# Attention by pairs of heads, with plain fp32 products on halves of TensorE

## The chip, the cores and the metric

The kernel runs on one core of one Trainium2 chip. The metric is the device time of one execution in microseconds (us). "Clock" is the clock that TensorE was granted, as a share of 2.4 GHz; its lower level is 0.5 (1.2 GHz).

## The reference, cut to what matters

Three stages follow each other: causal attention with a memory term, a mixture of eight experts with balanced gates, and a second, sparse mixture. Only the first is touched by the change.

```python
B, H, S, D = (4, 8, 576, 64)
...
scores = scale * np.matmul(q, k.transpose(0, 1, 3, 2))
causal = np.triu(np.ones((S, S), dtype=bool), k=1)
scores = np.where(causal, -1000000000.0, scores)
scores = scores - scores.max(-1, keepdims=True)
a = np.exp(scores)
a /= a.sum(-1, keepdims=True) + 1e-09
local = np.matmul(a, v)
...
q_p = phi(q)
mem_ret = np.einsum('bhsd,bhde->bhse', q_p, M_prev)
mem_norm = np.einsum('bhsd,bhd->bhs', q_p, z_prev)[..., None] + 1e-06
mem_out = mem_ret / mem_norm
g = 1.0 / (1.0 + np.exp(-beta))[None, :, None, None]
return (g * mem_out + (1 - g) * local).astype(np.float32)
```

There are 32 heads (4 batches of 8) of 576 queries and keys with 64 features each. All of it is fp32.

## The kernel before, in words

**Tiles.** A head's 576 queries are five tiles: 64, then four of 128. Causality leaves them 64, 192, 320, 448 and 576 keys, 1600 columns of scores in all (the last tile is cut into 288 and 288).

**Steps of a head.** q and k arrive transposed and doubled, so that each fills 128 partitions. `k_high` (ScalarE) rounds k to fp32r, `k_low` (VectorE) keeps what was lost, `q_high` (VectorE) rounds q, and `q_low` (GpSimd, for the first two heads VectorE if it is free) replaces the lower 64 partitions by q's lost part. `scores` multiplies this stack of both parts with k's high and then k's low part: two fp32r products over 128 rows for each tile. `rowmax` (VectorE) masks, scales, finds the row's bound and writes the scores to SBUF (tile `pe`); `exp` (ScalarE) works in place and sums the rows; `mem` (GpSimd) writes 64 columns of the memory term in front. `transposes` (TensorE, into PSUM tiles `t`) and `evac` (ScalarE or VectorE, whichever the planner picks) turn the result over into `pt`. `pv` then multiplies `pt` with `vm`, which holds M_prev and v of one head and zeros in the other 64 columns, so that two heads of a pair add up in one PSUM tile `o` of 128 partitions (head 0 in the upper half, head 1 in the lower). `finish` (VectorE) scales `o` into x once in a pair, with `factors` (TensorE) and `factors_out` (ScalarE) turning the scales over first. `phi_exp`, `phi`, `phi_z` and `mem_norm` prepare the memory term of a pair.

**Order.** The class `List` is a planner: every step has engines with assumed costs, steps that it comes after, buffers that it takes and gives, and an urgency from the table `AT` (head number times `PER`, plus an offset). It walks through an assumed time, starts on each free engine the most urgent step that can go, and records the instructions in that order. The chip runs each engine in that order and waits on semaphores. The gate's logits for the next stage (`logits`, 8 columns each) are woven in when the heads that they need are done. When the last `pv` is through, the experts' products (L607) begin.

Of the kernel before, what the change touches and what calls it, by code (L numbers as in the profile page):

```python
# [25 lines left out]
QR = [64] + [P] * (NQ - 1)  # L26
NK = [q0 + qr for q0, qr in zip(Q0, QR)]
PO = [sum(n + 64 for n in NK[:i]) for i in range(NQ)]
PW = PO[-1] + NK[-1] + 64
# [82 lines left out]
class Attention:  # L112
    def __init__(self, tc, ctx, io, ident, x):
# [12 lines left out]
        self.pt = pool("a_pt", 2)  # L126
# [15 lines left out]

        self.vm = [[cst.tile([P, NQ, P], F32, name=f"vm{j}{u}") for u in range(2)] for j in range(2)]
        for j in range(2):
            z = slice(64, P) if j == 0 else slice(0, 64)
            for u in range(2):
                nc.gpsimd.memset(self.vm[j][u][:, :, z], 0.0)
# [11 lines left out]
    def load(self, n):  # L159
        nc, io = self.nc, self.io  # L160
        q2 = self.ld.tile([P, S], F32, name="q2")
        k2 = self.ld.tile([P, S], F32, name="k2")
        nc.sync.dma_start(q2, io["qT2"][n])
        nc.sync.dma_start(k2, io["kT2"][n])
        self.raw[n] = (q2, k2)

    def load_pair(self, pr):
        nc, io = self.nc, self.io
        b, h = divmod(2 * pr, H)
        qn = self.mp.tile([P, 2, NQ, D], F32, name="qn", bufs=3)  # L170
        zb = self.mp.tile([P, 2, D], F32, name="zb", bufs=3)
# [4 lines left out]
    def load_v(self, n):  # L176
        j = n % 2
        self.nc.sync.dma_start(
            self.vm[j][n // 2 % 2][:, :, j * 64:j * 64 + 64], self.io["vm"][n].rearrange("(t p) d -> p t d", p=P))

    def make(self, n):

        st = self.st[n] = dict(
            qs=self.qk.tile([P, S], F32R, name="qs"), kh=self.qk.tile([P, S], F32R, name="kh"),
            kl=self.qk.tile([P, S], F32R, name="kl"), vm=self.vm[n % 2][n // 2 % 2],
            nb=self.sm.tile([P, NQ], F32, name="nb"), nb2=self.sm.tile([P, 1], F32, name="nb2"),
            sums=self.sm.tile([P, NQ], F32, name="sums"))
        st["q2"], st["k2"] = self.raw.pop(n)
# [63 lines left out]
    def rowmax(self, n, i):  # L252
# [3 lines left out]
        if i == 0:  # L256
            s["pe"] = self.pp.tile([P, PW], F32, name="pe")
# [1445 lines left out]
```

## Time and profile before

| | |
|---|---|
| median of 3 runs | 2170.3 us (2167.3 to 2186.7) |
| the profiled execution's own time | 2165.1 us |
| its span | 2163.4 us |
| attention: first score product to first expert product | 11.37 to 276.90 us |
| TensorE, VectorE, ScalarE, GpSimd busy over the span | 98%, 72%, 38%, 30% |

A busy share of TensorE counts products that stand in its pipeline, so it doesn't say that columns stream all the time; what a product costs is read from the start of one to the start of the next.

### The profile page before, as it was taken

Reading aid. Unit: us, or ns where it says so; the run is one execution under the profiler, and the core shown is the slowest. Engines: PE = TensorE matmul, PEld = TensorE weight load, DVE = VectorE, ACT = ScalarE, POOL = GpSimd, SP = SyncE. Lnnn points to the kernel's source line nnn. Section 1 sums busy time; section 2 is a strip of 40 time slices with the busy share of each in tenths; the row PEclk is TensorE's granted clock in tenths of the full one; section 3 lists DMA queues with packets and bytes.
Section 4 is the critical chain, followed back from the end, with each engine's and each line's share of the span. In section 5 each row is a group of like instructions: output and inputs, shape, how many; then the busy total and the mean of one; then the engine's idle time right before and its main releaser. Section 6 shows DMA issues by size and latency. Waiting matters only on the chain. (4 is left out here: it accounts for less than half of the span.)

```text
span 2163.4 us, 33548 instructions
## 1 busy us (share of the span) xinstructions
PE 2119.6 (98%) x11986; PEld 1831.9 (85%) x11986; DVE 1550.4 (72%) x3252; ACT 820.3 (38%) x1964; POOL 642.1 (30%) x721
## 2 busy tenths in 40 slices
PE   7999999999999999999999999999999999999998
PEld 5776778889988988898888898899889888788886
DVE  7789858777777777777777777777777777534463
ACT  6777742323322322232433232223223322334463
POOL 6678732222222222222412222222222223311121
PEclk9999999999999999999999999999999999999999
DMA  5444311111111111111211211111111111134551
GB/s 157 128 121 107 86 49 40 40 40 49 50 40 45 44 50 40 50 48 41 83 40 40 88 41 49 40 50 49 40 39 50 49 39 64 55 117 149 198 179 54
DMA packets 129411, 147.81 MB, mean 68 GB/s; under 512 B 48714, under 2 KB 83530, under 8 KB 129232
## 3 DMA queue, kind: packets, MB, share of 16 engines
q1 hardware_dynamic: 125312, 136.11, 19.9%
q0 software_dynamic: 3920, 9.44, 1.4%
q8 instruction: 96, 1.57, 0.3%
q14 instruction: 83, 0.68, 0.1%
HBM read 205.30 MB, written 10.75 MB: 100 GB/s over the span
## 5 line engine op out<-in xcount | busy, mean ns | idle before, releaser
L607 PE MATMUL pm<-xch,w1h 128*128 128x288 f32 (+2 forms) x1792 | 535.5, 299 | 3.4 <-DVE u L620 2.7
L607 PE MATMUL pm<-xch,w1l 128*128 128x288 f32 (+2 forms) x1792 | 530.1, 296 | 3.7 <-DVE w1l L578 3.7
L607 PE MATMUL pm<-xcl,w1h 128*128 128x288 f32 (+2 forms) x1792 | 529.3, 295 | 0.0
L687 DVE SCALAR_TENSOR_TENSOR acc<-psy,pr,acc 128x512 f32<-128x512 f32 x504 | 378.0, 750 | 155.2 <-PE psy L678 145.0
L676 PE MATMUL psy<-w2h,h 128*128 128x512 f32 x1152 | 459.3, 399 | 0.4 <-ACT h L634 0.4
L678 PE MATMUL psy<-w2h,h 128*128 128x512 f32 x1152 | 457.2, 397 | 0.0
L677 PE MATMUL psy<-w2l,h 128*128 128x512 f32 x1152 | 457.2, 397 | 0.0
L620 DVE TENSOR_TENSOR u<-pm,u 128x288 f32<-128x288 f32 (+2 forms) x640 | 290.4, 454 | 120.1 <-PE pm L607 99.9
L607 PEld LDWEIGHTS pm<-xch,w1h 128*128 128x128 f32 x1792 | 338.5, 189 | 9.5 <-DVE u L620 5.0
L607 PEld LDWEIGHTS pm<-xch,w1l 128*128 128x128 f32 x1792 | 338.9, 189 | 4.4 <-DVE w1l L578 4.4
L607 PEld LDWEIGHTS pm<-xcl,w1h 128*128 128x128 f32 x1792 | 338.9, 189 | 2.7
L572 POOL TENSOR_TENSOR s<-raw 128x256 f32<-128x256 f32 x128 | 95.8, 748 | 816.3 <-issue 800.9
L634 ACT ACTIVATE h<-u 128x288 fp32r<-128x288 f32 (+4 forms) x512 | 181.9, 379 | 357.3 <-DVE u L620 357.0
L644 ACT ACTIVATE u<-pm 128x288 f32<-128x288 f32 (+2 forms) x128 | 51.5, 402 | 683.2 <-PE pm L607 683.2
L638 DVE SCALAR_TENSOR_TENSOR h<-u,h 128x288 fp32r<-128x288 f32 (+4 forms) x512 | 258.8, 535 | 69.6 <-ACT h L634 63.5
L678 PEld LDWEIGHTS psy<-w2h,h 128*128 128x128 f32 x1152 | 217.3, 189 | 54.9 <-DVE h L638 1.6
L676 PEld LDWEIGHTS psy<-w2h,h 128*128 128x128 f32 x1152 | 217.4, 189 | 50.0 <-ACT h L634 1.0
L677 PEld LDWEIGHTS psy<-w2l,h 128*128 128x128 f32 x1152 | 217.3, 189 | 49.0
L578 POOL TENSOR_TENSOR w2l<-raw,w2h 128x1024 fp32r<-128x1024 f32 x64 | 154.5, 2414 | 308.6 <-ACT w2h L575 303.8
L332 PE MATMUL o<-pt,vm 128*128 128x512 f32 (+3 forms) x320 | 126.9, 486 | 0.0
L270 ACT ACTIVATE pe<-pe,nb 64x64 f32<-64x64 f32 (+4 forms) x160 | 88.8, 555 | 34.7 <-DVE nb L261 33.6
L300 PEld LDWEIGHTS t<-ident,pe 128*128 128x128 f32 (+1 forms) x480 | 62.7, 146 | 41.2 <-issue 21.7
(300 smaller groups left out, 2971.3 us busy)
## 6 DMA issues: line engine op xcount, KB each, us to landing
rw<-in_moe_w_dram SPq DMA_DIRECT2D x94, 1024.0 KB
raw<-in_moe_w_dram SPq DMA_DIRECT2D x131, 512.0 KB
q<-in_qT_dram SPq DMA_DIRECT2D x32, 288.0 KB
k<-in_kT_dram SPq DMA_DIRECT2D x32, 288.0 KB
qn<-in_qn_dram SPq DMA_DIRECT2D x16, 320.0 KB
vm<-in_vm_dram SPq DMA_DIRECT2D x32, 160.0 KB
out_dram<-acc SPq DMA_DIRECT2D x18, 256.0 KB
zb<-in_z_prev_dram SPq DMA_DIRECT2D x16, 64.0 KB
```

What stands on the lines that cost most here:

```text
L270: nc.scalar.activation(pv, pv, AF.Exp, bias=s["nb"][:r, i:i + 1], scale=-1.0, accum_out=s["sums"][:r, i:i + 1])
L332: nc.tensor.matmul(o[:, 448 + q0:1024], v[:, kk, :], p[:, kk * 512 + q0:kk * 512 + S], start=first and kk == 0, stop=last and kk == NQ - 1)
L572: return lambda: nc.gpsimd.tensor_tensor(o, x, y, op)
L578: return lambda: eng.tensor_tensor(o, src, f32(h), ALU.subtract)
L607: nc.tensor.matmul(o, w, x, start=start and k == 0 and i == 0, stop=k == 1 and i == 2, skip_group_check=not start)
L620: nc.vector.tensor_tensor(o, a, b, ALU.add)
L634: nc.scalar.activation(o, src[:, i], AF.Relu)
L638: nc.vector.scalar_tensor_tensor(o, src[:, i], 0.0, f32(hi), ALU.max, ALU.subtract)
L676: nc.tensor.matmul(ps, hh[:, ts], h2[:, f, :], start=f == 0, stop=False)
L677: nc.tensor.matmul(ps, hh[:, ts], l2[:, f, :], start=False, stop=False)
L678: nc.tensor.matmul(ps, hl[:, ts], h2[:, f, :], start=False, stop=f == 1)
L687: nc.vector.scalar_tensor_tensor(a, ps, self.pr[:, j, e:e + 1], a, ALU.mult, ALU.add)
```

## The change

The two heads of a pair now go through together. q and k of a pair lie on top of each other: head 0 in partitions 0 to 63, head 1 in 64 to 127, without a copy. The steps `make`, `k_high`, `k_low`, `q_high` and `q_low` are gone. `scores` is one plain fp32 product per head and tile, over 64 rows: head 0 uses the upper half of TensorE's rows, head 1 the lower, one right behind the other, into two PSUM tiles. `pv` is one fp32 product per head and block of keys with 64 columns of weights (`vm` has no zeros any more): head 0 in the first half of TensorE's columns, head 1 in the second, again one right behind the other, and it runs for both heads of a pair at once. The first query tile is handled as 128 rows up to the transposes, so the two transposes over 64 rows are gone too. PSUM is dealt out anew: four tiles for scores in place of three, two for transposes in place of three. `pe` has six tiles of one query tile each in place of two of a whole head. The planner's costs, urgencies and rings are new.

```diff
+SC = [(i, k0, k1) for i in range(NQ) for k0, k1 in ([(0, NK[i])] if NK[i] <= 512 else [(0, NK[i] // 2), (NK[i] // 2, NK[i])])]
+TC = [(0, 0, 1), (1, 0, 2), (2, 0, 3), (3, 0, 4), (4, 0, 4), (4, 4, 5)]
...
-        self.qk = pool("a_qk", 2)
-        self.pp = pool("a_p", 2)
+        self.pp = pool("a_p", self.RINGS["pe"])
-        self.ps_s = pool("a_pss", 3, space=PSUM)
-        self.ps_t = pool("a_pst", 3, space=PSUM)
+        self.ps_s = pool("a_pss", 4, space=PSUM)
+        self.ps_t = pool("a_pst", 2, space=PSUM)
...
-        self.nc.scalar.activation(self.st[n]["kh"], self.st[n]["k2"], AF.Copy)
...
-        self.nc.vector.tensor_tensor(st["kl"], st["k2"], f32(st["kh"]), ALU.subtract)
...
-        self.nc.vector.tensor_copy(self.st[n]["qs"], self.st[n]["q2"])
...
-    def scores(self, n, i):
...
-            nc.tensor.matmul(o, qs[:, Q0[i]:Q0[i] + r], kh[:, k0:k1], start=True, stop=False)
-            nc.tensor.matmul(o, qs[:, Q0[i]:Q0[i] + r], kl[:, k0:k1], start=False, stop=True)
+    def scores(self, m, c):
+
+        nc = self.nc
+        q, k = self.raw["qk", m]
+        i, k0, k1 = SC[c]
+        for j in range(2):
+            r = slice(j * 64, j * 64 + 64)
+            o = self.ps_s.tile([P, 512], F32, name="s")[:, :k1 - k0]
+            nc.tensor.matmul(o, q[r, Q0[i]:Q0[i] + P], k[r, k0:k1], start=True, stop=True)
+            self.raw["s", 2 * m + j, c] = o
...
+    def pv(self, m, kk):
+        nc = self.nc
         if kk == 0:
-            nc.tensor.matmul(o[:, 448:512], v[:, 0, :], p[:, 0:64], start=first, stop=last)
+            self.o[m] = self.ps_o.tile([P, 1024], F32, name="o")
         q0 = max(Q0[kk], 64)
-        nc.tensor.matmul(o[:, 448 + q0:1024], v[:, kk, :], p[:, kk * 512 + q0:kk * 512 + S],
-                         start=first and kk == 0, stop=last and kk == NQ - 1)
+        cols = ([(0, 64)] if kk == 0 else []) + [(q0, S)]
+        for a, b in cols:
+            for j in range(2):
+                o = self.o[m][j * 64:j * 64 + 64]
+                nc.tensor.matmul(o[:, 448 + a:448 + b], self.vm[j][m % 2][:, kk, :],
+                                 self.pt[j][m % 2][:, kk * 512 + a:kk * 512 + b],
+                                 start=kk == 0, stop=b == 64 or kk == NQ - 1)
...
-            self.nc.tensor.transpose(t[:, 0, :64], rsb[:64, 0, :], self.ident[:64, :64])
+            self.nc.tensor.transpose(t[:, 0, :], rsb[:, 0, :], self.ident)
...
+    RINGS = dict(qk=2, pair=2, s=2, pe=6, t=2, pt=2, o=1, rb=1)
+
+    PER = 11.33
...
+    T_S = (0.21, 0.42, 0.63, 0.85, 0.58, 0.58)
...
+    T_PV = (1.28, 0.96, 0.75, 0.53, 0.32)
...
-        li = List(dict(qk=2, pair=2, s=3, pe=2, t=3, pt=2, o=1, rb=1))
+        li = List(self.RINGS)
...
-        "qT2": np.concatenate([qT, qT], 1),
-        "kT2": np.concatenate([kT, kT], 1),
+        "qT": qT,
+        "kT": kT,
```

How the order of TensorE changes is seen in the middle of attention. Before, one head goes through products with V while the next is scored (`s` are scores, `t` transposes, `o` products with V, `rsb` the scales):

```order
L248 MATMUL s<-kh,qs 128x288
L249 MATMUL s<-kl,qs 128x288
L330 MATMUL o<-pt,vm_129 128x64
L332 MATMUL o<-pt,vm_129 128x512
L300 MATMUL t<-ident,pe 128x128 x5
L332 MATMUL o<-pt,vm_129 128x512
L248 MATMUL s<-kh,qs 64x64
L249 MATMUL s<-kl,qs 64x64
L332 MATMUL o<-pt,vm_129 128x384
```

After, on the same engine and at the same kind of place, with L219 the scores, L268 the transposes and L294 the products with V:

```order
L219 MATMUL s<-k,q 128x448 x2
L306 MATMUL t<-ident,rsb 128x128 x4
L294 MATMUL o<-pt_127,vm_123 64x64
L294 MATMUL o<-pt_129,vm_125 64x64
L294 MATMUL o<-pt_127,vm_123 64x512
L294 MATMUL o<-pt_129,vm_125 64x512
L219 MATMUL s<-k,q 128x288 x2
L294 MATMUL o<-pt_127,vm_123 64x512
L294 MATMUL o<-pt_129,vm_125 64x512
L308 MATMUL t<-ident,rsb 128x128
L268 MATMUL t<-ident,pe 128x128
L294 MATMUL o<-pt_127,vm_123 64x384
```

Each score row now has both heads (x2) and stands alone between transposes or products with V; each product with V is two rows of 64 partitions, one for each head, and no head's `pv` is apart from its partner's.

On VectorE before, the splits stand between two heads' row bounds (L261), here with an evacuation (L318) and the scales behind them:

```order
L261 ISA pe,nb<-s,mask,nb_512 128x288
L261 ISA nb 128x1
L200 CAST qs<-q_548 128x576
L197 TENSOR_TENSOR kl<-k_549,kh 128x576
L318 COPY pt<-t 128x4x128
L284 TENSOR_SCALAR rs<-sums,cpos 128x5
L285 RECIPROCAL rs<-rs 128x5
```

After, at that place (L235 the row bounds of the pair's two heads, L281 an evacuation):

```order
L235 ISA pe,nb<-s,mask,nb_647 128x288
L235 ISA nb 128x1
L235 ISA pe,nb<-s,mask,nb_658 128x288
L235 ISA nb 128x1
L281 COPY pt_127<-t 128x3x128
L255 TENSOR_SCALAR rs<-sums,cpos 128x5
L256 RECIPROCAL rs<-rs 128x5
```

The two splits are gone, and two heads' row bounds alternate.

## Rows read from the trace of the kernel before

**Rows 1.** The page, busy time of each engine over the span.
```profile
PE 2119.6 (98%) x11986; PEld 1831.9 (85%) x11986; DVE 1550.4 (72%) x3252; ACT 820.3 (38%) x1964; POOL 642.1 (30%) x721
```

**Rows 2.** Lines of `finish` on VectorE: count, shortest/median/longest ns, first to last start.
```profile
L362 DVE TENSOR_TENSOR xA<-o,rb x4: 744/752/758, 40.1 to 82.8; 128x576 f32<-128x576 f32 x4
L362 DVE TENSOR_TENSOR xB<-o,rb x4: 745/748/758, 169.0 to 217.7; 128x576 f32<-128x576 f32 x4
...
L365 DVE TENSOR_TENSOR xA<-o,rb x4: 678/684/692, 103.2 to 145.9; 128x512 f32<-128x512 f32 x4
L365 DVE TENSOR_TENSOR xB<-o,rb x4: 651/680/692, 240.0 to 277.2; 128x512 f32<-128x512 f32 x4
```

**Rows 3.** Stretches: us; busy PE, PEld, DVE, ACT, POOL; granted clock; DMA share; GB/s.
```profile
54.40:82.80 28.40, 28.08 (x162) 20.63 (x160) 24.01 (x82) 24.48 (x69) 22.78 (x37) 1.00 0.52 135
103.20:145.90 42.70, 42.38 (x245) 31.08 (x242) 37.59 (x122) 35.84 (x100) 32.37 (x51) 1.00 0.49 130
150.00:169.00 19.00, 19.00 (x106) 15.89 (x105) 13.24 (x36) 10.72 (x29) 10.60 (x17) 0.82 0.24 61
169.00:217.70 48.70, 44.70 (x249) 31.45 (x247) 45.50 (x125) 38.35 (x106) 41.47 (x55) 1.00 0.46 119
```

**Rows 4.** Who TensorE waited for, 103.2 to 145.9 us.
```profile
PE t L300 <- POOL pe L277: 0.3, 1, 0.3
```

**Rows 5.** TensorE in order of time: start us, us, instruction, shape, count.
```profile
107.81 0.81 PE L332 MATMUL o<-pt,vm 128*128 128x384 f32 x2
108.55 0.27 PE L345 MATMUL t<-ident,rsb 64*128 64x64 f32 x1
108.75 0.24 PE L248 MATMUL s<-kh,qs 128*64 128x64 f32 x1
...
108.89 0.68 PE L332 MATMUL o<-pt,vm 128*128 128x256 f32 x2
...
112.53 0.29 PE L248 MATMUL s<-kh,qs 128*128 128x288 f32 x1
112.66 0.30 PE L249 MATMUL s<-kl,qs 128*128 128x288 f32 x1
112.79 0.49 PE L300 MATMUL t<-ident,pe 128*128 128x128 f32 x3
113.12 1.02 PE L332 MATMUL o<-pt,vm 128*128 128x512 f32 x2
113.98 0.60 PE L300 MATMUL t<-ident,pe 128*128 128x128 f32 x4
114.42 0.81 PE L332 MATMUL o<-pt,vm 128*128 128x384 f32 x2
115.06 0.71 PE L300 MATMUL t<-ident,pe 128*128 128x128 f32 x5
```

**Rows 6.** VectorE's, ScalarE's and GpSimd's lines of the splits, 30 to 210 us.
```profile
L197 DVE TENSOR_TENSOR kl<-k,kh 128x576 fp32r<-128x576 f32 x23 | 20.6, 897 | 0.0
L200 DVE CAST qs<-q 128x576 fp32r<-128x576 f32 x22 | 14.3, 650 | 0.0
...
L192 ACT ACTIVATE kh<-k 128x576 fp32r<-128x576 f32 x22 | 14.9, 676 | 1.8 <-PE s L248 1.6
...
L204 POOL TENSOR_TENSOR qs<-q,qs 64x576 fp32r<-64x576 f32 x23 | 36.1, 1570 | 3.8 <-PE t L345 1.1 <-DVE qs L200 0.5 <-DVE nb L261 0.5
```

**Rows 7.** Evacuations of four transposes, the costliest form on ScalarE and on VectorE.
```profile
L320 ACT ACTIVATE pt<-t 128x512 f32<-128x512 f32 x35 | 20.5, 585 | 4.4 <-PE t L300 4.1
...
L318 DVE COPY pt<-t 128x512 f32<-128x512 f32 x10 | 6.8, 684 | 0.4 <-PE t L300 0.4
```

**Rows 8.** In order of time: the start of attention and the start of the experts' products.
```profile
8.36 0.68 ACT L192 ACTIVATE kh<-k 128x576 fp32r<-128x576 f32 x1 [2.79 <-DMA k<-in_kT_dram]
...
11.37 0.28 PE L248 MATMUL s<-kh,qs 128*64 128x64 f32 x1 [11.37 <-DVE qs L204]
...
276.90 0.38 PE L607 MATMUL pm<-xch,w1h 128*128 128x288 f32 x1
```

More of the change, by code (lines that the diff above doesn't have):

```diff
@@ L25 @@
 Q0 = [0] + [64 + P * i for i in range(NQ - 1)]
[L26 to L29, printed above, removed]
+NK = [q0 + (P if i else 64) for i, q0 in enumerate(Q0)]
+SC = [(i, k0, k1) for i in range(NQ) for k0, k1 in ([(0, NK[i])] if NK[i] <= 512 else [(0, NK[i] // 2), (NK[i] // 2, NK[i])])]
+TC = [(0, 0, 1), (1, 0, 2), (2, 0, 3), (3, 0, 4), (4, 0, 4), (4, 4, 5)]
+PW = S + 64
 PTW = 4 * 512 + S
@@ L141, in __init__ @@
         self.ieb = cst.tile([P, H], F32, name="ieb")
[L143 to L147, printed above, removed]
+        self.vm = [[cst.tile([P, NQ, D], F32, name=f"vm{j}{u}") for u in range(2)] for j in range(2)]
+        self.pt = [[cst.tile([P, PTW], F32, name=f"pt{j}{u}") for u in range(2)] for j in range(2)]
         self.raw, self.st, self.pair, self.o = {}, {}, {}, {}
@@ L322, in pv, with transposes @@
-    def pv(self, n, kk):
-        nc, s = self.nc, self.st[n]
-        if n % 2 == 0 and kk == 0:
-            self.o[n // 2] = self.ps_o.tile([P, 1024], F32, name="o")
-        o = self.o[n // 2]
-        first, last = n % 2 == 0, n % 2 == 1
-        v, p = s["vm"], s["pt"]
+    def transposes(self, n, c):
+        i, k0, k1 = TC[c]
+        pe = self.st[n]["pe", i]
+        t = self.st[n]["t", c] = self.ps_t.tile([P, 4, P], F32, name="t")
+        for kk in range(k0, k1):
+            self.nc.tensor.transpose(t[:, kk - k0, :], pe[:, kk * P:(kk + 1) * P], self.ident)
@@ new lines, in evac @@
+    def evac(self, n, c, eng):
+        i, k0, k1 = TC[c]
+        r, a = (P if i else 64), k0 * 512 + Q0[i]
+        pt = self.pt[n % 2][n // 2 % 2]
+        t = self.st[n].pop(("t", c))[:, :k1 - k0, :r]
+        if k1 == k0 + 1:
+            o = pt[:, a:a + r].unsqueeze(1)
+        else:
+            o = pt[:, a:a + (k1 - k0) * 512].rearrange("p (k q) -> p k q", q=512)[:, :, :r]
+        if eng == "DVE":
+            self.nc.vector.tensor_copy(o, t)
+        else:
+            self.nc.scalar.activation(o, t, AF.Copy)
@@ L366, in finish @@
             self.nc.vector.tensor_tensor(x[:, 2 * S - 64:], o[:, 448:512], rb[:, :64], ALU.mult)
-    PER, TILE, ROW = 6.64, 0.844, 0.539
-    AT = dict(load=-14.32, load_v=-6.07, pair=-16.92, prep=-9.4, phi=-5.96, phi2=-8.0, phi_z=-7.95, mem_norm=-6.5,
-              scores=-4.5, rowmax=-2.42, exp=1.5, mem=-1.01, transposes=2.9, evac=8.8, pv=12.31, norm=6.2,
-              factors=6.74, finish=13.09, logits=29.65)
-    EITHER = (0, 1)
+    RINGS = dict(qk=2, pair=2, s=2, pe=6, t=2, pt=2, o=1, rb=1)
@@ new lines @@
+    PER = 11.33
+    AT = dict(load=-33.43, load_v=10.5, pair=-43.18, phi=-32.57, phi2=-5.64, phi_z=-40.05, mem_norm=-1.04, scores=-4.58, rowmax=4.76,
+              exp=12.59, mem=-39.71, transposes=1.76, evac=14.2, pv=13.73, norm=17.79, factors=14.55, finish=8.1, logits=40.02)
+    T_S = (0.21, 0.42, 0.63, 0.85, 0.58, 0.58)
+    T_MAX, T_EXP = (0.28, 0.40, 0.55, 0.68, 0.50, 0.55), (0.50, 0.60, 0.70, 0.82, 0.93)
+    T_T = (0.11, 0.22, 0.33, 0.44, 0.44, 0.11)
+    T_EA, T_ED = (0.20, 0.38, 0.48, 0.58, 0.58, 0.27), (0.20, 0.42, 0.55, 0.68, 0.68, 0.28)
```

234 lines of the change are left out of this document (90 added, 144 removed).

## The prediction

> **What bounds the kernel now.** I read first who finishes a pair and when. `finish` runs once for each pair, and its starts lie 42.7 us apart for three pairs in two calm stretches, so 14.2 us a pair [rows 2]; a third stretch took 48.7 us, the last one 37.2 us, in which no new heads are prepared. The 16 pairs and what lies between them fill 11.37 to 276.90 us [rows 8], an eighth of the span; everything behind that is the experts, which the change doesn't touch. Next I asked which engine fills a pair. Busy shares alone say TensorE: 42.38 of 42.70 us in the stretch from 103.2, against 37.59 for VectorE and 35.84 for ScalarE [rows 3], and over the whole span it is 98% [rows 1]. A busy TensorE need not stream, so I checked with waits and with a count. The waits show one of 0.3 us in those three pairs [rows 4]. The count goes by starts [rows 5]: a fp32 product of 512 columns holds the next one back 0.86 us (113.12 to 113.98), one of 384 columns 0.64 us; that is 1.68 ns a column. A fp32r product of 288 columns takes 0.13 us (112.53 to 112.66), 0.45 ns a column. Four transposes take 0.44 us (113.98 to 114.42), 0.11 us each. A transpose over 64 rows is dearer: it lets the next one start after 0.20 us (108.55 to 108.75), and the 384 columns in front of it take 0.74 us in place of 0.64 us. For a pair:
>
> - products with V: 2 heads x 1856 columns x 1.68 ns = 6.2 us
> - scores: 2 heads x 1600 columns x 2 products x 0.45 ns = 2.9 us
> - transposes: 2 x (14 x 0.11 + 0.30) = 3.7 us
> - scales: 4 x 0.11 + 0.30 = 0.7 us
>
> The sum is 13.5 of 14.2 us. TensorE's columns bound the pair; 0.7 us is left for loads of weights and handing over, and I carry it over unchanged. In the stretch from 169.0 VectorE was busy 45.50 of 48.70 us [rows 3]: there parts of x for the experts are split too, and VectorE sets the pace for a while.
>
> **The change part by part.** *The splits* go: 2 x (0.897 + 0.650) = 3.1 us of VectorE a pair, 2 x 0.676 = 1.35 us of ScalarE, 2 x 1.570 = 3.1 us of GpSimd [rows 6]. None is on the path in the calm stretches, so by itself this gives nothing there. It gives room: from 12.5 and 11.9 us a pair (a third of the stretch from 103.2 in [rows 3]) VectorE and ScalarE come to 9.4 and 10.6 us, and since an evacuation may go to either, to about 10.0 us each. That is the floor under a faster TensorE. Halved loads of q and k are costed at nothing; the DMA share in those stretches is 0.49 [rows 3].
>
> *Products with V.* Two products of 64 columns of weights stand in place of two of 128 with zeros. If head 1's streams beside head 0's, a pair costs 1856 x 1.68 ns = 3.1 us, if it streams behind it, 6.2 us as now. *Scores.* Two fp32 products over 64 rows each: beside each other 1600 x 1.68 ns = 2.7 us a pair, behind each other 5.4 us. No row shows two halves at work at once, so both ends stand as bounds. I take "beside each other": the two have their own rows or columns of the array, their own partitions and PSUM places, and in the rows they share nothing but the order of instructions. This is the choice on which the forecast rests.
>
> The Trainium skill, page "TensorE: Matmul & The Clock Gate", section "Part 3: Packing small matmuls — row/col tiling", has products on different parts of the array run at once, each further one adding about 4 ns; no run here shows it yet, and by it the two terms would be those that I take.
>
> *Transposes and scales.* All are full now: (30 + 5) x 0.11 = 3.85 us in place of 4.4 us.
>
> *Going from full array to halves and back.* The transpose over 64 rows shows a price [rows 5]: 0.10 us in front and at least 0.20 - 0.11 = 0.09 us behind, so 0.2 us for each stay. The order after has six separate stays of scores in a pair: 1.2 us. For halves of columns the nearest row is the first tile's score over 64 columns, 0.14 us for both its products (108.75 to 108.89), which shows hardly any such price; the other bound is the 0.2 us of the rows. Five stays of `pv` cost 0 to 1.0 us; I take 0.5 us, nearer to the row of the same kind.
>
> The sum: 3.1 + 2.7 + 3.85 + 1.2 + 0.5 + 0.7 = 12.1 us a pair, over the floor of 10.0 us, against 14.2 us. Sixteen pairs give 16 x 2.1 = 34 us.
>
> *Start and end.* At present k has landed at 8.36 us, and the first score waits until 11.37 us for four splits in a chain [rows 8]. Without them it could start 3 us earlier, but the first transposes still need the memory term of the pair; I take 2 us. At the end both heads' products with V come behind the last evacuation, 3.6 us in place of one head's 3.1 us; this 0.5 us is inside that rounding.
>
> From 2165.1 us of the profiled execution that is 2165 - 34 - 2 = 2129 us. The median of the runs shown lies 5 us above the profiled execution; I keep the number of the execution.
>
> **The rivals.**
>
> *In order, half beside half.* A fp32 product is two instructions (x2 at one call in [rows 5]), the second with the other part of the weights; each starts when the one before is through, as the starts show. For two heads the order is then A1, A2, B1, B2. If no product may start ahead of one in front of it, B1 starts with A2, and B2 is alone: three quarters of the serial time. Scores 4.0, V 4.7, the rest 6.25 (3.85 + 1.2 + 0.5 + 0.7): 14.95 us a pair, 0.75 us more than now, 16 x 0.75 - 2 = +10 us: 2175 us. For it speaks that all starts of TensorE in [rows 5] follow the order; against it that nothing there had two halves to choose from. The same section of the page on TensorE says that products start and end strictly in the program's order and that only loads of weights are pulled ahead; by that rule the time would be this rival's. The trace agrees as far as it goes: its starts are in order.
>
> *Serial halves, slower.* If the second head's product waits for the first to be through, at scores and at V, a pair takes 5.4 + 6.2 + 6.25 = 17.9 us: 16 x 3.7 - 2 = +57 us, 2222 us. It is the other side of one mechanism: with 14.2 us to keep, scores and V may take 7.95 us; they are 5.8 us side by side and 11.6 us serial. So if less than about 63% of one head's time is hidden beside the other's, the kernel gets slower. For it speaks that the rows show a price for touching halves at all; against it that all operands are apart.
>
> *The halves work, but PSUM or the vector engines hold.* Transposes have two PSUM tiles now, not three. Filling one takes 0.60 us until its end [rows 5], emptying it 0.585 us on ScalarE or 0.684 us on VectorE [rows 7]; a pair has 14 such rounds of at most 1.2 to 1.3 us, and two tiles share them, so 7 x 1.25 = 8.75 us plus waits. With 0.5 us of waiting in each round, in the queue of a ScalarE that is 10.6 us busy, it becomes 12.3 us, with 0.64 us 13.2 us. At 13.2 us a pair the gain is 16 x 1.0 + 2 = 18 us: 2147 us. TensorE would then show waits at transposes, behind which scores and products with V are queued.
>
> **How the numbers follow.** Side by side 0.55, half beside half 0.27, serial 0.10, held by PSUM or the vector engines 0.08. The forecast's own range is 2110 us (no price for halves of columns, none of the 0.7 us left) to 2142 us (full price and 0.3 us more of waiting). The range of 2108 to 2180 us takes in the half-and-half case and the held one and leaves the serial one out. About 1%, 22 us, is what a measurement of this kernel can tell. Faster by more: nearly all of the first case and some of the last, 0.57. Within: most of the half-and-half case and the rest of the held one, 0.29. Slower: serial and the upper end of half-and-half, 0.14.
>
> **What would show it.** In the trace after, head 1's score should start within some hundredths of a microsecond of head 0's, and one pair of 448 columns should take about 0.75 us to the next step; 1.1 us means half beside half, 1.5 us serial. The starts of `finish` should be 12.1 us apart, VectorE and ScalarE busy for some 10 us of it, and the first expert product should start 36 us earlier. The prediction is wrong if the time between a product on halves and its neighbours is more than 0.2 us a stay, or if the clock falls more often: in the stretch with logits it was 0.82 [rows 3], and a TensorE that streams fewer columns could be granted the lower level in more places.

## The result, and the profile after

The changed kernel takes 2151.7 us in the median (2150.5 to 2153.3, four runs) against 2173.1 us (2167.3 to 2186.7, four runs) for the kernel before on the same chip. The ratio is 0.9893, its 95% interval 0.9845 to 0.9941: faster by 1.1%. The forecast was 2129 us, 22.6 us lower. The medians lie 21.4 us apart, the two profiled executions 11.8 us (2165.1 and 2153.3 us): the one before is shorter than all four runs of its kernel, the one after is the longest of its four, so the account below, which is of those two, leaves about half of the medians' difference open. At the mean clock of the profile before (0.990, a span of 2163.4 us) one run of the changed kernel had a span of 2148.8 us, 14.6 us less.

**Where the time came from.** `finish` after, which answers to [rows 2] (count, shortest/median/longest ns, first to last start):

```profile
L325 DVE TENSOR_TENSOR xA<-o,rb x4: 754/755/758, 33.7 to 73.9; 128x576 f32<-128x576 f32 x4
L325 DVE TENSOR_TENSOR xB<-o,rb x4: 751/754/758, 153.7 to 203.1; 128x576 f32<-128x576 f32 x4
...
L328 DVE TENSOR_TENSOR xA<-o,rb x4: 687/688/692, 91.9 to 135.8; 128x512 f32<-128x512 f32 x4
L328 DVE TENSOR_TENSOR xB<-o,rb x4: 680/682/691, 222.0 to 260.6; 128x512 f32<-128x512 f32 x4
```

The starts alternate (33.7, 45.4, 62.2, 73.9), so pairs are taken by twos: 33.7 to 62.2 is 28.5 us, 45.4 to 73.9 also 28.5 us, 14.25 us a pair at full clock and with no logits in between. Before it was 14.2 us. **A calm pair has become no shorter at all.** TensorE's first score product and the first expert product, in order of time, the answer to [rows 8]:

```profile
7.52 2.25 PE L219 MATMUL s<-k,q 64*128 64x64 f32 x9 [7.52 <-DMA k<-in_kT_dram]
...
260.40 0.40 PE L572 MATMUL pm<-xch,w1h 128*128 128x288 f32 x1
```

Attention takes 252.9 us in place of 265.5 us, and the experts start 16.5 us earlier. The starts of `finish` in both traces, with the instructions of the logits counted (two for each of their products, 0.11 us each) and low clock counted as half lost, say where:

| stretch | before, us | after, us | logits | low clock, us | rest gained, us |
|---|---|---|---|---|---|
| first score to 1st `finish` | 28.7 | 26.2 | 0, 0 | 3.4, 6.8 | 4.2 |
| 1st to 5th | 63.1 | 58.2 | 32, 8 | 3.4, 0 | 0.5 |
| 5th to 9th | 65.8 | 61.8 | 40, 32 | 6.8, 3.4 | 1.4 |
| 9th to 13th | 71.0 | 68.3 | 32, 48 | 6.8, 6.8 | 4.5 |
| 13th to 16th | 37.2 | 38.6 | 0, 16 | 0, 0 | 0.4 |

The gain is 3.9 us of earlier start, 4.2 us in the first pair, 4.5 us in the four pairs among which x is split for the experts, 1.7 us of less low clock, and 2.3 us in the eleven others.

Counting low clock as half lost is an assumption, and in the first pair a run speaks against it. The version with the logits apart (below) has the changed kernel's instructions in the same order up to 107 us. It had no low clock in its first pair and took no less for it, 27.0 us against 26.2 us with 6.8 us of low clock:

```profile
7.81:34.80 26.99, 26.07 (x125) 15.35 (x126) 16.29 (x71) 18.60 (x58) 11.85 (x25) 1.00 0.45 118
```

So for the first pair the plain difference, 28.7 - 26.2 = 2.5 us, is what is shown; the less low clock elsewhere is then worth up to 3.4 us in place of 1.7 us.

The stretch in which VectorE set the pace [rows 3] no longer shows it as busy; windows after, columns as in [rows 3]:

```profile
33.70:62.20 28.50, 26.64 (x167) 13.38 (x167) 20.04 (x74) 21.82 (x64) 13.81 (x29) 1.00 0.36 93
...
153.70:203.10 49.40, 46.81 (x267) 24.95 (x269) 33.23 (x108) 34.76 (x95) 24.43 (x42) 0.93 0.27 69
```

33.23 of 49.40 us, against 45.50 of 48.70 us. In the calm stretch VectorE and ScalarE are busy 10.0 and 10.9 us a pair, about the 10 us that were forecast.

**The halves do run side by side.** Within a row of the timeline the single starts can be found by asking for ever narrower windows. The two V products of both heads, 512 columns each, in the windows 99.570 to 99.5735, 99.573 to 99.60, 100.044 to 100.0505 and 100.055 to 100.06:

```profile
99.57 0.64 PE L294 MATMUL o<-pt,vm 128*64 128x512 f32 x1
99.57 0.65 PE L294 MATMUL o<-pt,vm 128*64 128x512 f32 x2
99.57 1.07 PE L294 MATMUL o<-pt,vm 128*64 128x512 f32 x3
99.57 1.08 PE L294 MATMUL o<-pt,vm 128*64 128x512 f32 x4
```

Each of the two products is two instructions. One has started by 99.5735, two soon after, three by 100.0505, all four by 100.06: head 1's first product starts some 7 ns behind head 0's, and the two second products start 7 ns apart too, 0.48 us later. In the program both of head 0's instructions stand before head 1's first. With both heads on the same rows (an experiment below) the four starts lie 0.24 to 0.35 us apart, so two that start 7 ns apart belong to different heads. So A1 and B1 run together, then A2 and B2, and the rival "in order, half beside half" has fallen.

**What they cost.** TensorE in order of time after, one pair's middle; it answers to [rows 5]:

```profile
37.77 0.33 PE L268 MATMUL t<-ident,pe 128*128 128x128 f32 x1 [0.58 <-ACT pt L283]
38.03 1.02 PE L219 MATMUL s<-k,q 64*128 64x448 f32 x4
38.98 0.66 PE L306 MATMUL t<-ident,rsb 128*128 128x128 f32 x4
39.57 1.20 PE L294 MATMUL o<-pt,vm 128*64 128x64 f32 x8
40.69 0.76 PE L219 MATMUL s<-k,q 64*128 64x288 f32 x4
41.38 1.08 PE L294 MATMUL o<-pt,vm 128*64 128x512 f32 x4
42.39 0.33 PE L308 MATMUL t<-ident,rsb 128*128 128x128 f32 x1
...
42.75 0.87 PE L294 MATMUL o<-pt,vm 128*64 128x384 f32 x4
43.55 0.33 PE L268 MATMUL t<-ident,pe 128*128 128x128 f32 x1
43.81 0.65 PE L294 MATMUL o<-pt,vm 128*64 128x256 f32 x4
44.39 0.44 PE L268 MATMUL t<-ident,pe 128*128 128x128 f32 x2
44.76 0.44 PE L294 MATMUL o<-pt,vm 128*64 128x128 f32 x4
45.13 0.76 PE L219 MATMUL s<-k,q 64*128 64x288 f32 x4
```

A row's price is its start to the next row's. A pair of scores of 448 columns takes 0.95 us (38.03 to 38.98), 0.20 us over its 0.75 us of columns; a pair of V products of 512 columns 1.01 us (41.38 to 42.39), 0.15 us over its 0.86 us. A single transpose between two stays takes 0.26 us (37.77 to 38.03, and 43.55 to 43.81) in place of 0.11 us; that 0.15 us is partly the way in (0.09 us) and partly the first full product behind (0.06 us). So a stay of scores costs 0.35 us and one of V 0.30 us. With six and five of them a pair pays 6 x 0.35 + 5 x 0.30 = 3.6 us. Where one stay follows another directly, as at 40.69, 41.38 and 45.13, the 0.15 us is not paid between them. Counted from start to start over the two pairs from 33.7 to 62.2 us, columns are 9.6 us a pair, waits 0.9 us and all else 3.7 us, so the sum of the prices comes out right even so.

TensorE's waits after, 33.7 to 91.9 us, four pairs (the answer to [rows 4]; us, times, longest):

```profile
PE t L268 <- ACT pt L283: 2.2, 5, 0.6
PE t L306 <- ACT pt L283: 0.7, 1, 0.7
PE t L268 <- DVE pt L281: 0.4, 2, 0.2
PE t L268 <- POOL pe L249: 0.2, 1, 0.2
```

3.5 us, 0.9 us a pair, nearly all of it transposes that wait for an evacuation. With 9.65 us of columns as forecast, 3.6 us of stays and 1.0 us of waits and the rest, a pair is 14.25 us.

**What is given back.** Of the 16.5 us, 12.9 are left at the fiftieth expert product. Windows of the hand-over, after:

```profile
260.40:264.20 3.80, 1.86 (x10) 1.16 (x8) 2.33 (x4) 0.72 (x2) 3.44 (x6) 1.00 0.00 0
264.20:281.30 17.10, 15.66 (x67) 15.31 (x68) 8.84 (x15) 5.54 (x12) 7.96 (x6) 0.50 0.10 31
```

and before:

```profile
276.90:283.10 6.20, 2.88 (x17) 1.95 (x15) 4.49 (x5) 1.78 (x3) 5.82 (x6) 1.00 0.00 0
283.10:289.90 6.80, 5.92 (x26) 5.92 (x27) 2.70 (x6) 2.15 (x5) 3.23 (x5) 0.50 0.22 77
```

In both the experts begin with TensorE half idle, since their first weights are split just then (the same waits for `w1l`, in the same order). Behind that the clock stays at its lower level for 17.1 us after, for 6.8 us before. The 10.3 us more are worth up to 5 us of streaming.

### The profile page after: what moved, and what is told of

Read it like the earlier page. It is cut to its first block, busy times and chain, and to the rows that moved or that the text cites. A ratio compares the mean times of both kernels' runs of the same rounds, so it can differ in the third digit from the quotient of the medians.

```text
span 2151.6 us, 33371 instructions
## 1 busy us (share of the span) xinstructions
PE 2102.9 (98%) x11986; PEld 1771.2 (82%) x11986; DVE 1500.1 (70%) x3182; ACT 804.2 (37%) x1937; POOL 574.6 (27%) x654
## 4 chain that ended last, share of the span: by engine, by line
PE 89%; DVE 3%; DMA 3%; issue 2%; ACT 1%; POOL 0%; SPq 0%; POOLq 0%; DVEq 0%; ACTq 0%
PE pm L572 32%; PE psy L641 12%; PE psy L643 12%; PE psy L642 12%; PE s L219 3%; PE o L294 3%; PE t L268 3%; DMA out_dram<-o,idx 1%; PE psh L1442 1%; PE psh L1440 1%; PE psh L1441 1%; PE psy L1464 1%; PE psy L1465 1%; PE psy L1466 1%; DMA xg<-out_dram,idx 1%
## 5 line engine op out<-in xcount | busy, mean ns | idle before, releaser
L572 PEld LDWEIGHTS pm<-xch,w1h 128*128 128x128 f32 x1792 | 339.5, 189 | 10.3 <-DVE u L585 5.9
L537 POOL TENSOR_TENSOR s<-raw 128x256 f32<-128x256 f32 x128 | 95.5, 746 | 819.9 <-issue 800.9
L603 DVE SCALAR_TENSOR_TENSOR h<-u,h 128x288 fp32r<-128x288 f32 (+4 forms) x512 | 258.1, 533 | 69.1 <-ACT h L599 63.1
L268 PEld LDWEIGHTS t<-ident,pe 128*128 128x128 f32 x480 | 54.5, 146 | 64.4 <-issue 25.4
L235 DVE CUSTOM_DVE_ANT_0 pe<-s,mask 128x64 f32<-128x64 f32 (+4 forms) x160 | 65.9, 425 | 49.1 <-PE t L268 38.6
L268 PE MATMUL t<-ident,pe 128*128 128x128 f32 x480 | 85.2, 296 | 12.3 <-ACT pt L283 8.3
```

Of the source, the lines that this page charges most:

```text
L235: nc.vector.tensor_tensor_reduce(s["pe", i][:, 64 + k0:64 + k1], self.raw.pop(("s", n, c)), self.mask[:, m0 + k0:m0 + k1], -0.125, s["nb2" ...
L268: self.nc.tensor.transpose(t[:, kk - k0, :], pe[:, kk * P:(kk + 1) * P], self.ident)
L537: return lambda: nc.gpsimd.tensor_tensor(o, x, y, op)
L572: nc.tensor.matmul(o, w, x, start=start and k == 0 and i == 0, stop=k == 1 and i == 2, skip_group_check=not start)
L603: nc.vector.scalar_tensor_tensor(o, src[:, i], 0.0, f32(hi), ALU.max, ALU.subtract)
```

## The experiments

Each edit is one to the changed kernel. Where it changes the planner's steps, costs or buffers, the planner makes a new order with the urgencies that were searched for the changed kernel (for the new plan below they were searched again). Only with the stays doubled and in their control do VectorE, ScalarE and GpSimd keep the changed kernel's order throughout, and with the logits apart up to 107 us. In all other runs a total holds the edit and a new order in one; the rows of the timeline don't mix them. TensorE's waits for `mem` on GpSimd are one sign of such an order: 0.2 us over the attention in the changed kernel, 10.5 to 15.6 us in three of these runs.

"Attention" is first score to first expert product in the profiled execution (252.9 us in the changed kernel, 265.5 us before), "low" the time in it at TensorE's lower clock (17.1 and 20.5 us).

### One stay for V

```diff
-            for kk in range(NQ):
-                add(("pv", m, kk), dict(PE=self.T_PV[kk]), self.pv, (m, kk), o + at["pv"] + kk * 0.5,
...
+            add(("pv", m, NQ - 1), dict(PE=sum(self.T_PV) - 0.43), lambda m: [self.pv(m, kk) for kk in range(NQ)], (m,), o + at["pv"],
...
```

> The changed kernel with all five blocks of a pair's products with V as one step of the planner, so TensorE goes to halves of its columns once in a pair and not five times. Changed kernel: 252.9 us from first score to first expert product, 2151.7 us. Theory A (each stay on halves costs about 0.3 us, and TensorE's time sets the pair): four stays fewer, 4 x 0.3 x 16 = 19 us less, 234 us of attention and 2133 us. Theory B (the two PSUM tiles of transposes and the engines that empty them set the pair): TensorE is away from transposes for 3.5 us at a time, so nothing is gained; 253 to 265 us of attention, 2152 to 2164 us.

2180.7 us, ratio to before 1.0044 (1.0027 to 1.0061); attention 276.4 us, low 58.0 us. TensorE's timeline shows a pair's whole V in one row:

```profile
54.74 3.35 PE L294 MATMUL o<-pt,vm 128*64 128x64 f32 x24
58.02 0.55 PE L268 MATMUL t<-ident,pe 128*128 128x128 f32 x3
```

TensorE's waits in attention, 30 to 285 us, the two largest:

```profile
PE t L268 <- POOL pe L249: 12.9, 8, 5.8
PE t L268 <- ACT pt L283: 7.5, 21, 0.7
```

The 24 instructions (12 products) take 3.28 us for 3.12 us of columns: one price of 0.16 us in place of five. In the changed kernel the same work takes 1.12 + 1.01 + 0.80 + 0.58 + 0.37 = 3.88 us in five rows, so four stays less save 0.6 us inside and another four times 0.15 us around. The price is confirmed, the gain is not: waits come to over 20 us, and the clock falls more often. One reading is that the five blocks of V had filled the time in which transposes wait, and in one lump fill none of it. It isn't shown: the longest wait (5.8 us, up to 102.96 us) ends with `mem`, and ahead of its memory-term work GpSimd itself had stood idle for 3.5 us, up to 99.42 us, until VectorE had made `phi`, which comes late in the new order. The numbers expected were missed either way.

### V over all columns

```diff
...
-                o = self.o[m][j * 64:j * 64 + 64]
-                nc.tensor.matmul(o[:, 448 + a:448 + b], self.vm[j][m % 2][:, kk, :],
+                o = self.o[m]
+                nc.tensor.matmul(o[:, 448 + a:448 + b], self.vm[m % 2][:, kk, :],
...
-    T_PV = (1.28, 0.96, 0.75, 0.53, 0.32)
+    T_PV = (2.05, 1.71, 1.28, 0.85, 0.43)
```

The products of the two heads have 128 columns of weights, both heads' V beside each other, so what is added up mixes the heads; the work on TensorE is that of V before. The planner is told the longer costs.

> The changed kernel with the products with V over all 128 columns, one head behind the other, and the scores still on halves. The columns that would have to be zero hold the other head's V, so the two heads' results are mixed; read the attention's time alone. Theory A: products with V take 6.2 in place of 3.1 us a pair, five stays of 0.3 us are saved, 1.6 us x 16 = 26 us more than 252.9 us, so 279 us from first score to first expert product. Theory B: TensorE has 1.5 us a pair of slack, and most of it is taken up; 253 to 262 us.

2184.7 us (one run), attention 283.6 us, low 23.9 us. V of 512 columns for both heads now takes 1.72 us (64.33 to 66.05) in place of 1.01 us:

```profile
64.33 1.88 PE L295 MATMUL o<-pt,vm 128*128 128x512 f32 x4
66.05 0.38 PE L269 MATMUL t<-ident,pe 128*128 128x128 f32 x2
```

Sixteen pairs lose 3.1 us of columns each and save five stays of 0.30 us: 16 x 1.6 = 26 us, and 6.8 us more of low clock cost up to 3.4 us. Measured are 30.7 us. This sets V's columns and V's stays against each other in one number, and it is close to what the rows give and to the 279 us of theory A.

### Both heads' scores on the same rows

```diff
-            r = slice(j * 64, j * 64 + 64)
+            r = slice(0, 64)
...
-    T_S = (0.21, 0.42, 0.63, 0.85, 0.58, 0.58)
+    T_S = (0.32, 0.74, 1.17, 1.60, 1.06, 1.06)
```

Head 1's scores are computed from head 0's q and k, and the planner is told the longer costs.

> The changed kernel with both heads' scores on the same half of TensorE's rows, so that they can't run beside each other; head 1 is scored with head 0's q and k, so read the attention's time alone. If the two heads ran wholly beside each other before, a pair of 448 columns takes 1.5 us to the next step in place of 0.75 us, and a pair of heads 2.7 us more: 16 x 2.7 = 43 us more than 252.9 us, 296 us (theory A). With 1.5 us a pair of slack on TensorE (theory B) about 20 us more, 273 us.

2249.4 us (one run), attention 347.7 us, low 102.4 us. A pair of scores of 288 columns takes 1.17 us (63.38 to 64.55); in the changed kernel it takes 0.69 us (40.69 to 41.38 above):

```profile
63.38 1.24 PE L219 MATMUL s<-k,q 64*128 64x288 f32 x4
64.55 1.46 PE L268 MATMUL t<-ident,pe 128*128 128x128 f32 x8
```

The 0.48 us more is one head's 288 columns at 1.68 ns: on the same rows the second head waits for the first, on rows of its own it does not. Over the attention that is 16 x 2.7 = 43 us; 85 us more of low clock cost up to 43 us more, and of the 94.8 us measured some 9 us are left to waits. Both totals expected (296 and 273 us) were missed by far; the local row decides here, not the total.

### Score tiles and transpose tiles

```diff
-        self.ps_s = pool("a_pss", 4, space=PSUM)
-        self.ps_t = pool("a_pst", 2, space=PSUM)
+        self.ps_s = pool("a_pss", 2, space=PSUM)
+        self.ps_t = pool("a_pst", 4, space=PSUM)
...
-    RINGS = dict(qk=2, pair=2, s=2, pe=6, t=2, pt=2, o=1, rb=1)
+    RINGS = dict(qk=2, pair=2, s=1, pe=6, t=4, pt=2, o=1, rb=1)
```

> The changed kernel with PSUM dealt out the other way: two tiles for scores, four for transposes (the planner's rings follow). Theory A: nothing gained at the transposes beyond their measured waits of about 0.8 us a pair, and the scores of the next tile can't start before both row bounds are through, so 253 to 275 us of attention. Theory B: the transposes' waits go, 1.0 us x 16 = 16 us less, 237 us, 2136 us.

The control has two score tiles and two transpose tiles.

> The changed kernel with two PSUM tiles for scores and the two for transposes left as they are: the control of the run with two and four (302.2 us from first score to first expert product). If transposes' tiles set the pair (theory B), two in place of four must cost much: 330 us or more. If they don't (theory A: price of the stays, with too few tiles for scores as the cause of that run's loss), within 10 us of 302 us.

With two and four 2202.2 us, ratio 1.0156 (1.0129 to 1.0183), attention 302.2 us, low 95.6 us; with two and two 2222.8 us (one run), attention 318.9 us, low 112.6 us. Waits of TensorE with two and four, 30 to 309 us:

```profile
PE s L219 <- DVE nb L235: 12.1, 18, 1.9
PE t L268 <- POOL pe L249: 10.5, 13, 2.0
```

With four transpose tiles no wait for an evacuation is left. Two more of them are worth 16.7 us where scores have two tiles; two more score tiles are worth 66 us where transposes have two. So the transposes' tiles do hold something, and the scores' tiles, which the forecast didn't weigh, hold more; both totals contain low clock (17 us between the first two, 95.5 us between the control and the changed kernel), and counted at half it leaves 8 and 18 us. Neither run came out as expected: 302.2 us lies above both theories of the first, 318.9 us between the two of its control. Four and four was not tried.

### Three stays for V

```diff
+    PG = ((0,), (1,), (2, 3, 4))
...
+            for i, g in enumerate(self.PG):
+                add(("pv", m, g[-1]), dict(PE=sum(self.T_PV[kk] for kk in g)), lambda m, g: [self.pv(m, kk) for kk in g], (m, g),
...
```

> The changed kernel with the last three blocks of products with V (384, 256 and 128 columns) as one step, the first two alone: three stays on halves of columns a pair and not five, with 1.3 us of TensorE's time as the longest step. Theory A: 2 x 0.3 x 16 = 10 us less than 252.9 us of attention, 243 us, if the short blocks were not what filled TensorE's waits. Theory C (formed from the run with one stay: short blocks of V stand in the gaps while transposes wait, and a TensorE with gaps gets the lower clock): the saving is used up by longer gaps, 250 to 262 us.

2152.4 us, ratio 0.9932 (0.9911 to 0.9953), attention 254.0 us, low 30.7 us. The attention lies in theory C's range. The first finishes come at 30.9, 44.6, 58.8 and 72.6 us: two pairs take 27.9 and 28.0 us, 14.0 us a pair. That is 0.3 us less than 14.25; two stays cost 0.6 us. It is lost again between the fifth and the ninth `finish`, mostly in one place. TensorE's timeline of the place:

```profile
138.02 4.48 PE L483 MATMUL t<-wg,xA 128*128 128x8 f32 x32
142.35 1.85 PE L483 MATMUL t<-wg,raw 128*128 128x8 f32 x8
```

Windows of the place, columns as in [rows 3]:

```profile
138.00:140.80 2.80, 2.80 (x27) 2.78 (x25) 1.76 (x4) 2.77 (x4) 0.49 (x1) 1.00 0.28 63
140.80:157.90 17.10, 12.76 (x49) 8.50 (x48) 9.94 (x35) 6.91 (x18) 7.88 (x12) 0.50 0.19 54
```

The new order has put 40 of the logits' small instructions (20 products) in a row, and behind the first 27 of them the clock falls for 17.1 us.

### Stays doubled, and the control

Three V blocks of a pair are cut in two, with one small product over the whole array (8 columns, two instructions) between the pieces, which adds three stays.

```diff
+        if 0 < kk < 4:
+            c = (q0 + S) // 2
+            cols = cols[:-1] + [(q0, c), (c, S)]
...
+            if 0 < kk < 4 and a == q0:
+                nc.tensor.matmul(self.o[m][:, 0:8], self.ident, self.ident[:, 0:8], start=True, stop=True)
```

> The changed kernel with three blocks of V (512, 384 and 256 columns) cut in two and a product of 8 columns over the full array in between, into a part of PSUM that nobody reads: three more stays a pair and three small products. To be held against the run with the same cuts and the small product behind both parts. Theory A: each stay costs 0.3 us, 3 x 0.3 x 16 = 14 us more than that run. Theory B: TensorE has slack, under 6 us more.

The control has the same pieces and the same small product, but it stands behind both (`b == S` in place of `a == q0`).

> The control of the run with three more stays: the same cuts and the same small product over the full array, but behind both parts, where TensorE goes back to the full array or on to scores anyway. Against the changed kernel it has three small products of 0.11 us and three cuts a pair, and where scores follow, a stay of their own is not added: 3 x 0.15 x 16 = 7 us more than 252.9 us by theory A, under 4 us by theory B.

2174.0 us and 2170.3 us (one run each); attention 276.1 us with 10.2 us low, and 269.4 us with 27.3 us low. The timeline of TensorE with stays doubled, a block of 384 columns:

```profile
46.26 0.55 PE L297 MATMUL o<-pt,vm 128*64 128x192 f32 x4
46.73 0.39 PE L301 MATMUL o<-ident 128*128 128x8 f32 x2
47.05 0.55 PE L297 MATMUL o<-pt,vm 128*64 128x192 f32 x4
47.53 0.33 PE L268 MATMUL t<-ident,pe 128*128 128x128 f32 x1
```

and of the control:

```profile
60.89 0.87 PE L297 MATMUL o<-pt,vm 128*64 128x192 f32 x8
61.69 0.39 PE L301 MATMUL o<-ident 128*128 128x8 f32 x2
61.94 0.31 PE L268 MATMUL t<-ident,pe 128*128 128x128 f32 x1
```

From the block's first start to the step behind it: 1.27 us against 1.05 us, so one stay more is 0.22 us here. By `finish`, four pairs take 63.9 us (36.7 to 100.6) and 61.2 us (34.4 to 95.6), so 0.68 us a pair for three stays, 0.23 us each. The total would have said 6.7 us for 48 stays, 0.14 us each; the control's low clock hides the rest. Counted at half, the difference is 15 us, 0.32 us a stay. So the difference of the totals, 6.7 us, lies between the two theories (14 us, under 6 us), and the rows decide for a price. The control itself takes 16.5 us more than the changed kernel, above both numbers expected of it (7 and 4 us); 5 us of that can be low clock. The price lies between 0.22 us (one stay more, by itself) and 0.35 us (scores, in their place).

### Logits apart

The logits' products get urgencies 1.4 us apart, to keep them out of rows.

```diff
-                    j, u = p * NTP + c, last * at.PER + at.AT["logits"]
+                    j, u = p * NTP + c, last * at.PER + at.AT["logits"] + 1.4 * c
```

> The changed kernel with the logits' urgencies 1.4 us apart, so that the planner strews the logits (8 columns each) among other products in place of up to 16 in a row. If rows of logits are what makes TensorE's clock fall in attention (it fell at 110.6 us after such a row and at 172.0 us after another, 10 us at the lower level), it stays up there: about 5 us less than 252.9 us of attention, 248 us, 2147 us. If the clock falls for the waits and the half-empty array in general, it falls at other places: 250 to 256 us.

The same with three stays for V:

> Three stays of the products with V in place of five, and the logits' urgencies 1.4 us apart. With three stays alone the pairs at full clock were 14.05 us, and the clock was low for 30.7 us of attention, 17.1 of them after 40 products of logits and a wait of 3 us behind them. If the stays' price holds and the row of logits was the cause of the low clock: 16 x 0.5 = 8 us less than 252.9 us and 5 us less for the clock, 240 us, 2139 us. If joining blocks of V leaves gaps that pull the clock down wherever the logits stand: 250 to 256 us.

2160.5 us, ratio 0.9947 (0.9927 to 0.9967), attention 261.0 us, low 27.3 us; with three stays 2156.4 us, ratio 0.9937 (0.9914 to 0.9961), attention 253.7 us, low 27.3 us. By the medians both are slower than the changed kernel, but their intervals overlap with its 0.9845 to 0.9941; the first ran from 2152.9 to 2165.8 us, and the profile is of 2165.8 us. Its 261.0 us miss both numbers expected, the 253.7 us with three stays lie in the second.

The edit did less than it was meant to. The planner still put two tiles' logits together, 16 instructions in a row; the first such row in the run with five stays:

```profile
113.92 1.92 PE L481 MATMUL t<-wg,xA 128*128 128x8 f32 x16
```

There is another at 205.25 us, and with three stays one of 24 at 199.35 us. The clock falls behind these rows too (at 116.2 and 208.4 us; with three stays at 204.3 us), but of the 27.3 us of low clock with five stays only 6.8 us stand behind a row of 16, and 20.5 us begin elsewhere, at 194.7, 222.0 and 259.6 us. So rows of logits are not the only place where the clock falls; whether they bring it down can't be told from runs that still have them. With three stays the twelfth `finish` comes at 195.4 us, 7.7 us ahead of the changed kernel's 203.1 us, and nothing of that is left at 261.4 us.

### A new plan

Three stays, the price of a stay given to the planner, a bias against going to halves and back, and a newly searched table of urgencies.

```diff
...
+MODE, PEN, TURN = dict(scores="rows", pv="columns"), 1.48, 0.13
...
+                    k = min(go, key=lambda k: steps[k][3] + (PEN if MODE.get(k[0]) != mode else 0))
...
+                if e == "PE" and MODE.get(k[0]) != mode:
+                    mode, cost = MODE.get(k[0]), cost + TURN
...
```

> Three stays, logits apart, and the planner told what the traces show: 0.13 us for each change between the full array and halves, products on halves at their measured times, 0.55 us for a tile's logits, a preference for staying in the same shape, and urgencies searched anew for that. Order and costs alone; the work is the changed kernel's. Theory A (the price of stays that the planner didn't know of): 14.5 us a pair becomes 13.5 us, 16 us less than 252.9 us, 237 us of attention, 2136 us, and it beats both kernels. If waits that no planner's cost describes (queues of the vector engines, the clock) decide: within 5 us of 252.9 us.

2154.3 us, ratio 0.9922 (0.9896 to 0.9947), attention 253.3 us, low 30.7 us. The window from its twelfth `finish` to its fifteenth:

```profile
194.30:249.70 55.40, 50.89 (x275) 28.00 (x272) 36.59 (x115) 36.65 (x100) 33.95 (x46) 0.82 0.30 82
```

and of the changed kernel from its twelfth to its fifteenth:

```profile
203.10:253.10 50.00, 46.56 (x300) 25.73 (x299) 39.00 (x129) 39.28 (x111) 34.25 (x49) 1.00 0.33 91
```

At 194.3 us it is 8.8 us ahead. In the next three pairs 5.4 us of that go, 55.4 us against 50.0 us, with 20.5 us at the lower clock where the changed kernel has none; the rest goes in the last pair (11.3 against 7.5 us). The attention is what the second theory expected. The profile is of an execution of 2157.9 us, and two of its four runs took 2149.5 and 2150.6 us, at a mean clock of 0.987 and 0.986 in place of 0.982; so the clock's share is not the same in every execution. No version here is measurably faster than the changed kernel.

### The splits put back as idle work

The four splits of each head run on ScalarE, VectorE and GpSimd as before, into one buffer that all four share and no product reads.

```diff
...
+            for j, n in enumerate(heads):
+                p = o + j * self.PER / 2 - 9.4
+                add(("k_high", n), dict(ACT=0.57), self.k_high, (n,), p, after=[("load", m), ("q_low", n - 1)])
+                add(("k_low", n), dict(DVE=0.67), self.k_low, (n,), p + 0.5, after=[("k_high", n)])
+                add(("q_high", n), dict(DVE=0.37), self.q_high, (n,), p + 0.5, after=[("k_low", n)])
+                add(("q_low", n), dict(POOL=1.36), self.q_low, (n,), p + 0.5, after=[("q_high", n)])
```

> The changed kernel with the four splits of each head put back as idle work: ScalarE, VectorE (twice) and GpSimd do them at the old costs and urgencies, in a buffer that nobody reads; TensorE's products, order of dependences and PSUM are those of the change. Set against each other by the stretches of the two traces with logits and low clock taken out, a pair without logits costs 14.2 to 14.3 us before and after, and the change gained 4.5 of some 7 us in the four pairs behind the ninth finish, where x's parts are split. Theory A (the gain of those pairs is VectorE's and GpSimd's relief, not TensorE's columns): those four pairs go from 68.3 us to 71 to 74, pairs in calm stretches lengthen by 0 to 0.5 us, and attention comes to 257 to 266 us, the time to 2156 to 2166. Theory B (the relief is worth nothing because TensorE's halves set the pace everywhere): attention within 2 us of 252.9, the time 2150 to 2154. If calm pairs lengthen by over 1 us each, the vector engines are the bound of the change there too.

2190.4 us, ratio 1.0104 (1.0083 to 1.0125), attention 287.1 us, low 47.8 us. TensorE's largest wait, 30 to 295 us:

```profile
PE t L281 <- POOL pe L262: 15.6, 8, 7.1
```

and GpSimd's own largest wait about the longest of these, 134 to 145.5 us:

```profile
POOL qe L212 <- DVE qn L207: 5.4, 1, 5.4
```

34 us more, far above theory A's range of 257 to 266 us, of which 31 us more of low clock make up to 15 us. Theory A had the sign but not the place: by the accounting of the table above, the pairs up to the ninth `finish` lengthen by 1.0 to 1.4 us each, the four behind it by 0.4 us, the last three by 0.9 us. The first pair takes 1.9 us more. By its number the third case that was named is met, calm pairs over 1 us longer, but not its cause. VectorE and ScalarE are busy only 74 and 72% of the attention (213.05 and 206.08 of 287.10 us). The transposes wait for `mem` on GpSimd (15.6 us in place of 0.2 us), in part because it stands behind `q_low`; before the longest wait ended (7.1 us, at 145.00 us), GpSimd had stood idle for 5.4 us itself, up to 140.41 us, until VectorE had made `phi`, which comes late in the new order. So the run prices the idle work together with an order whose urgencies were not made for it, and with a buffer that ties the four steps of all heads together. How much a table of urgencies made for this load would give back was not tried, and what the splits alone cost is not shown.

## Why the prediction was right, and where it was not

The kernel is faster, and the range held; the size did not. The medians' 21.4 us lie just under the 22 us that the forecast took as the limit for "faster by more". That the range held is in good part luck: of the 34 us that were put on the pairs, calm pairs gave nothing, and what gain there is came from other terms.

- **Side by side: right.** The second head's start lies 7 ns behind the first (forecast: some hundredths of a microsecond). The columns of a pair are the 9.65 us of the sum, and the two experiments that take the halves away lose what they should (0.48 us for 288 columns of scores; 29 of 30.7 us for V, with the clock). The two serial rivals have fallen. The Trainium skill, page "TensorE: Matmul & The Clock Gate", section "Part 3: Packing small matmuls — row/col tiling", gives about 4 ns for each further product; the traces have 7 ns. The Trainium skill says in the same section that products start and end strictly in the program's order; these traces don't agree, since head 1's first instruction starts 0.47 us ahead of head 0's second.
- **"Going from full array to halves and back": the step that failed.** The mechanism was named; the term was mis-sized. I took 0.2 us for a stay of scores and 0.1 us for one of V, 1.7 us a pair. They are 0.35 and 0.30 us, 3.6 us a pair. I had read the price before and behind a product over 64 rows, but not the one inside, and for columns I took 0.1 us, half of that, because a row of two fp32r products over 64 columns showed hardly any price; that row was no guide to these products. The text's own condition for being wrong, a stay of more than 0.2 us, was met. The missing 1.9 us a pair are 30 us, nearly the whole difference of 16 x 2.1 us.
- **The rest: 0.7 us carried over, 1.0 us measured.** The waits of 0.9 us a pair are those of the rival "held by PSUM": transposes waiting for an evacuation, with two tiles. It was true in kind and small in size.
- **"By itself this gives nothing": no run speaks against it for the calm stretch before, but it is too narrow.** The four pairs in which x is split gained 4.5 us, where VectorE had been busy 45.50 of 48.70 us and now is 33.23 of 49.40 us. That the splits' removal gave all of it is not shown: put back as idle work they take 1.6 us of it away (0.4 us a pair). In that run the whole attention is 34 us longer, so this order needs those engines' room, which the forecast counted as a floor only; how much a plan made for it would need is open.
- **Start: 2 us forecast, 3.9 us measured**, and the first pair is another 2.5 us shorter (4.2 us if its low clock counts as half lost, which a run with the same order doesn't bear out). I had no term for that. That two heads in one pass fill the pipeline sooner is a likely reason, not a shown one.
- **Clock: named as a risk, and it went both ways.** In attention 3.4 us less of low clock, at the hand-over 10.3 us more, which takes back 3.6 us.

By these prices V gained 3.1 - 5 x 0.30 = 1.6 us a pair, transposes and scales 0.55 us; scores lost 6 x 0.35 - 0.2 = 1.9 us, and waits 0.3 us. That is a calm pair of the same length as before, and the 11.8 us between the profiles are mostly start, first pair and the pairs with x's splits, less what the clock takes back. Open are three things: what the splits' removal is worth by itself; what brings the clock down between 195 and 250 us in the versions with fewer stays or logits apart (the runs show that it falls there, not why); and how much a planner that knew the clock could keep of the 0.3 us a pair that three stays save.

## What to carry to other kernels

Halves of the array really do double small products, but every stay has a price; so count the stays before you count the columns, and read the price inside a stay as well as around it. An edit that relieves an engine can be worth nothing in the old kernel's calm pairs and something in the new one; to price it, take it back in the new kernel, but with the order held or searched anew, or the run prices the order as well. And when small blocks are joined to save their price, look at what the new order does to the waits: here one stay in place of five saved its price in the row and lost it in the total.

## What was not expected of the hardware

- fp32 products of two heads on halves interleave by themselves: first instructions 7 ns apart, second instructions 7 ns apart and, at 512 columns, 0.48 us later, although the program has both of one head's first.
- A stay on halves costs 0.22 us by itself, 0.30 us (64 columns) and 0.35 us (64 rows) in its place; within one stay 24 instructions of different lengths cost 0.16 us over their columns.
- The lower clock came for 17.1 us behind 27 instructions of 8 columns in a row in one version, and for 3.4 us behind a row of 16 in another. It also came where no such row stood, and in two versions with the same order up to there the first pair had 6.8 us of it in one and none in the other, and was no longer for it (26.2 and 27.0 us).
